# Key blocks taken from the group right ahead, u loaded through another queue, and result banks in pairs: one change to a kernel of gated attention and experts

## The chip, the cores and the metric

The kernel runs on one core of a Trainium2 chip. The metric is the device time of one execution in microseconds (us). The time before is the median of three executions, 911.72 us (906.89 to 917.02). The execution that the profiler recorded is a separate one; its span is 944.3 us.

## The reference

Eight sequences of 2816 tokens go through a gated attention without softmax, and every token then through a dense two-layer net plus one of eight experts, chosen by a gate:

```python
scores = scale * np.matmul(z, z.transpose(0, 2, 1))     # z: 8 x 2816 x 64, scale = 1/2816
attn = np.maximum(scores, 0.0) ** 2
x = u * np.matmul(attn, v)                              # u, v: 8 x 2816 x 256
...
h_dense = np.maximum(x @ w1_dense, 0.0)                 # 256 -> 512
y_dense = h_dense @ w2_dense                            # 512 -> 256
expert_idx = np.argmax(x @ w_gate, axis=1)              # 8 experts
y_moe[mask] = gate_w[mask, None] * (np.maximum(x[mask] @ w1[e], 0.0) @ w2[e])
out = y_dense + y_moe
```

The scores are z times its own transpose. So the score of query i and key j is that of query j and key i, and a block of the attention matrix is the transpose of the block across the diagonal.

## The kernel before, in words

**Attention.** A sequence is 22 tiles of 128 tokens. Its query tiles are worked in six groups of 2, 4, 4, 4, 4 and 4 tiles (`groups`). For a group n the kernel keeps a buffer `A[n]` that holds, for all 22 key tiles, the squared and clipped scores of the group's queries; there are three such buffers, in turn. A buffer is filled in units. A unit is two key tiles (in groups of four query tiles): two score matmuls on TensorE (L353; 64 rows each, in the two halves of the array), a clip and scaling from PSUM into `r` (L370 on ScalarE or L372 on VectorE) and a square from `r` into `A` (L383 on ScalarE or L385 on VectorE). Units are issued in batches of up to three (`fill`, `scores`), as three PSUM pairs `psS` of two banks each are there for them.

Not all key blocks are computed. For group n the keys of group n - 2 of the same sequence (`far`) are the transposes of blocks that stand in `A[n - 2]` already, and are moved from there by DMA transposes on the Sync queue (`far_steps`, L414): one for each query tile of the target, 128 x 512 values at the most. `left[n]` lists the units that remain.

`av` then forms the products of one query tile with v: 22 matmuls of 128 x 256 (L486) into one of two single PSUM banks (`psY`). Between them it issues batches of scores for this group and the two next, and at three places in a tile it may issue one transpose from the list `turning`, if the planner reckons that its source is there. `gate_x` multiplies the result by u (L508, VectorE) into `pays` and starts a DMA transpose of it (L510, Sync queue), which the gate's logits need.

**The order.** TensorE, ScalarE, VectorE and the Sync queue run in the order in which the program issues to them. A small planner in the program picks that order: it keeps a clock `now`, assumed durations for each operation, and gives each clip and square to whichever of ScalarE and VectorE it reckons to be done first. GpSimd's order is left to the framework.

**Queues.** Loads of u (L140, 256 KB for two tiles) are on the Sync queue, as are all transposes. GpSimd issues the loads of v, of z (from the second sequence on) and of the weights, and the scatter of every tile's rows into a table `xs` sorted by expert (L620). A tile's rows in `pays` can be overwritten only once their scatter, 22 tiles earlier, has landed.

**Expert slots.** After attention come up to 92 slots of 256 tokens (`slot`). The first 70 (`NT1`) have one expert for all 256 tokens, the later ones one for each half. The last two are run only if the routing needs them. A slot s does, in this order on TensorE: the dense up-product of its tokens, the down-products of the second half of slot s - 2, its expert's up-product, and the down-products of the first half of slot s - 1 (`up`, L823; `half` and `down`, L831). ScalarE evicts up-products through a relu (L825). A half's two results, dense and expert, share one PSUM bank: the dense one is copied out (L843 on VectorE in the first 70 slots, L845 on ScalarE later), then VectorE adds the scaled expert one (L846), and GpSimd scatters the sum to the output (L848). `expert` copies the weights of the next slot's expert next to each other (L809, VectorE).

In this half all eight PSUM banks are one ring (`bank`): an up-product takes two banks, one for each pair of hidden chunks, each with a relu of its own; a half takes one bank. The attention's PSUM pools are closed before it (`part1`).

Of the kernel before, what the change touches and what calls it, by code (L numbers as in the profile page):

```python
# [15 lines left out]
P = 128  # L16
# [3 lines left out]
def kernel(  # L20
# [58 lines left out]

    part1 = ctx.enter_context(ExitStack())  # L80
    psS = part1.enter_context(tc.tile_pool(name="psS", bufs=NPAIR, space=bass.MemoryType.PSUM))
    psY = part1.enter_context(tc.tile_pool(name="psY", bufs=2, space=bass.MemoryType.PSUM))
    psR = []

    def bank():
        if not psR:
            part1.close()
            psR.append(pool("psR", 8, space=bass.MemoryType.PSUM))
        return psR[0].tile([P, 4 * P], F32, name="bank", tag="b")[:]
# [47 lines left out]
    def load_u(g):  # L137
        ut = aw.tile([P, 2, D], F32, name="ut", bufs=3)
        b, i = divmod(g, nK)
        nc.sync.dma_start(out=ut[:], in_=uf[:, b, i:i + 2, :])  # L140
        ut_of[g], ut_of[g + 1] = ut[:, 0, :], ut[:, 1, :]
# [177 lines left out]
    left, far, key_at = {}, {}, {}  # L319
    for n, (b, i0, w) in enumerate(groups):  # L320
        far[n] = [m for m in (n - 2,) if m >= 0 and groups[m][0] == b]
        turned = {k for m in far[n] for k in range(groups[m][1], groups[m][1] + groups[m][2])}
        ks = [k for k in range(0, nK, 2) if k not in turned]

        left[n] = [tuple(ks[x:x + 4 // w]) for x in range(0, len(ks), 4 // w)]
# [78 lines left out]
    def far_steps(a):  # L404

        n = a + 2
        if n >= len(groups) or far[n] != [a]:
            return []
        (b, i0, w), (_, j0, wj) = groups[n], groups[a]

        def step(i):
            assert n - 1 in A
            open_group(n)
            nc.sync.dma_start_transpose(out=A[n][:, j0:j0 + wj, i * P:(i + 1) * P],  # L414
                                        in_=A[a][:, i0 + i, :wj * P])
            if i == w - 1:
                for j in range(wj):
                    key_at[n, j0 + j] = now[0] + 10.0

        return [(a, lambda i=i: step(i)) for i in range(w)]  # L420
# [50 lines left out]
    def av(n, i):  # L471
# [7 lines left out]
        for x in range(nK):  # L479
            k = rest[0]  # L480
            if i == i0:

                k = min(rest, key=lambda k: (key_at.get((n, k), 9e9), k))
                need(n, k)
            rest.remove(k)
            nc.tensor.matmul(out=o[:], lhsT=A[n][:, k, (i - i0) * P:(i - i0 + 1) * P],  # L486
                             rhs=v_of[b][:, k, :], start=(x == 0), stop=(x == nK - 1))
            pe(0.1092)
            if x % 2 == 1:
                fill(n)  # L490
            if x % 7 == 3 and turning:
                t = can_turn(turning[0][0] + 2, turning[0][0])
                if t is not None and t <= now[0] and turning[0][0] + 1 in A:
                    turning.pop(0)[1]()
            if x == nK // 2 and b * nK + i > Q1 * G:
                one_scatter()
# [21 lines left out]
    def logits(q):  # L518
        n = sizes[q]
        if psR:  # L520
            lg = bank()[:, :G * E].rearrange("p (t e) -> p t e", e=E)
        else:
            lg = psS.tile([P, G, E], F32, name="lg", tag="s")
        lg_of[q] = lg[:, :n, :]
        for j in range(n):
            xT = xT_of.pop(starts[q] + j)
            for c in range(2):
                nc.tensor.matmul(out=lg[:, j, :], lhsT=xT[:, c, :],
                                 rhs=wg[:, c, :], start=(c == 0), stop=(c == 1))
# [24 lines left out]
    def route_pre(q):  # L554
        oh, ex = rs[q]
        if psR:
            pre = bank().rearrange("p (i x) -> p i x", i=2)
        else:
            pre = psS.tile([P, 2, E * G], F32, name="pre", tag="s")
# [253 lines left out]
    def up(xT, ws):  # L813

        n = 2 // len(ws)
        h = take("h")
        for f2 in range(2):
            h_ps = bank().rearrange("p (f h t) -> p f h t", f=2, h=2)
            for i, w1 in enumerate(ws):
                hs = slice(i * n, (i + 1) * n)  # L820
                for f in range(2):
                    for c in range(2):
                        nc.tensor.matmul(out=h_ps[:, f, hs, :], lhsT=w1(c, 2 * f2 + f),  # L823
                                         rhs=xT[:, hs, c, :], start=(c == 0), stop=(c == 1))
            nc.scalar.activation(h[:, 2 * f2:2 * f2 + 2, :],  # L825
                                 h_ps.rearrange("p f h t -> p f (h t)"), AF.Relu)
# [7 lines left out]
    def half(s, j):  # L834
# [4 lines left out]
        y = bank().rearrange("p (k d) -> p k d", d=D)  # L839
        down(y, 0, hd, lambda f: w2d[:, f, :], j)  # L840
        down(y, 1, he, lambda f: we[:, 2 * F + f * D:2 * F + (f + 1) * D], j)
        if s < NT1:
            nc.vector.tensor_copy(yd, y[:, 0, :])  # L843
        else:
            nc.scalar.copy(yd, y[:, 0, :])  # L845
# [21 lines left out]
    def slot(s, end):  # L867
# [12 lines left out]
        if s + 1 < NT and s + 1 not in wes:  # L880
# [129 lines left out]
    for s in range(NT - MAYBE + 2):  # L1010
# [4 lines left out]
        if s % 3 == 1:  # L1015
# [5 lines left out]
    with tc.If(n > NH - 2 * MAYBE):  # L1021
        for s in range(NT - MAYBE, NT + 2):
# [31 lines left out]
```

## Time and profile before

Busy time of the engines over the span of 944.3 us:

| engine | busy us | share | instructions |
|---|---|---|---|
| TensorE, matmuls (PE) | 901.0 | 95% | 8298 |
| TensorE, weight loads (PEld) | 698.5 | 74% | 8298 |
| VectorE (DVE) | 769.7 | 82% | 1563 |
| ScalarE (ACT) | 707.3 | 75% | 950 |
| GpSimd (POOL) | 464.8 | 49% | 434 |

The hardware queue, which Sync's transfers use, moved 67.37 MB in 221664 packets, the software queue of GpSimd 55.44 MB in 27616. The page gives a share for a whole span, though the two halves differ: attention runs from 11.6 to 585.9 us, the slots from 586.7 us on. So shares are best asked for by stretch. A group's line gives the line of the program, the engine, what is written from what, the number of instructions, busy us and the mean of one in ns, and after the bar the idle time just before them with what ended most of it. Matmuls overlap in the array, so the mean of one (274 ns for L486) is its latency; the distance from one to the next, a median of 109 ns, is read from the timeline.

### The profile page before, as it was taken

The numbers are of one execution on the slowest core, as the hardware profiler recorded it, in microseconds if no ns is written. First come the engines' busy times: TensorE is split into PE (matmuls) and PEld (weight loads), VectorE is DVE, ScalarE is ACT, GpSimd is POOL, SyncE is SP. The second block draws the span as 40 slices with busy tenths as digits, with TensorE's granted clock in tenths as the row PEclk, the third lists the DMA queues.
The fourth block names the chain that finished last, engine by engine and source line by source line (L and its number), as shares of the span: only waits on it lengthen the run. The fifth ranks groups of instructions, "written<-read, shape, count | busy, mean of one in ns | idle before, by whom it ended". The sixth has DMA issues, their size and how long they took to land.

```text
span 944.3 us, 23155 instructions
## 1 busy us (share of the span) xinstructions
PE 901.0 (95%) x8298; PEld 698.5 (74%) x8298; DVE 769.7 (82%) x1563; ACT 707.3 (75%) x950; POOL 464.8 (49%) x434
## 2 busy tenths in 40 slices
PE   8999999999999999999999999988998999999996
PEld 5677776767777777777777767877777888888885
DVE  7999998988998998998998985766775776676555
ACT  7998997987987988987988972545554655566764
POOL 2202544445544555554455454556655555556555
PEclk8999999999999999999999999999999999999998
DMA  6687799888797999789798563555543444344332
GB/s 142 127 140 140 138 189 147 145 167 159 144 156 156 148 170 168 141 159 173 133 176 159 125 132 84 106 126 117 114 99 103 111 110 114 101 97 102 90 90 65
DMA packets 249395, 124.28 MB, mean 132 GB/s; under 512 B 217022, under 2 KB 224446, under 8 KB 249280
## 3 DMA queue, kind: packets, MB, share of 16 engines
q1 hardware_dynamic: 221664, 67.37, 37.6%
q0 software_dynamic: 27616, 55.44, 28.6%
q8 instruction: 65, 1.06, 0.5%
q14 instruction: 50, 0.41, 0.2%
HBM read 61.54 MB, written 37.16 MB: 105 GB/s over the span
## 4 chain that ended last, share of the span: by engine, by line
PE 42%; issue 22%; DVE 14%; POOL 13%; DMA 6%; ACT 1%; POOLq 1%; SPq 1%; DVEq 0%; ACTq 0%
PE o L486 21%; PE bank L823 8%; POOL out_dram L848 8%; PE s L353 6%; PE bank L831 5%; DMA xs<-pays,pi 4%; POOL xs L620 4%; DVE r L372 3%; DVE A L385 3%; DVE pays L508 2%; DVE ring L809 1%; DVE ring L843 1%; DMA A<-A 1%; DVE zn L116 1%; DVE ring L846 1%
## 5 line engine op out<-in xcount | busy, mean ns | idle before, releaser
L486 PE MATMUL o<-vb,A 128*128 128x256 bf16 x3872 | 457.2, 274 | 6.8 <-DVE pays L508 3.6
L486 PEld LDWEIGHTS <-A 128*128 128x128 bf16 x3872 | 365.1, 98 | 108.0 <-issue 63.6
L620 POOL DMA_INDIRECT xs<-pays,pi x176 | 230.6, 1310 | 264.6 <-DVE pi L619 145.2
L370 ACT ACTIVATE r<-s 128x1024 f32<-128x1024 f32 x292 | 280.6, 1010 | 48.0 <-PE s L353 33.9
L825 ACT ACTIVATE ring<-bank 128x512 bf16<-128x512 f32 x360 | 193.7, 609 | 141.7 <-PE bank L823 100.5
L383 ACT ACTIVATE A<-r 128x1024 bf16<-128x1024 f32 (+1 forms) x235 | 238.4, 1047 | 12.2 <-DVE r L372 9.3
L385 DVE TENSOR_TENSOR A<-r 128x1024 bf16<-128x1024 f32 x197 | 235.4, 1214 | 0.6 <-ACT r L370 0.6
L848 POOL DMA_INDIRECT out_dram<-ring,me x140 | 146.5, 1046 | 111.6 <-DVE ring L846 72.8
L372 DVE TENSOR_SCALAR r<-s 128x1024 f32<-128x1024 f32 x140 | 170.2, 1218 | 7.8 <-PE s L353 5.2
L831 PEld LDWEIGHTS <-ring 128*128 128x128 bf16 x1440 | 139.7, 98 | 20.0 <-issue 3.9
L353 PE MATMUL s<-zT 64*128 64x512 bf16 (+1 forms) x944 | 122.6, 364 | 4.3 <-ACT zT L183 2.2
L843 DVE COPY ring<-bank 128x256 f32<-128x256 f32 x140 | 58.3, 416 | 70.3 <-PE bank L823 66.2
L823 PE MATMUL bank<-ring 128*128 128x256 bf16 (+1 forms) x880 | 98.5, 255 | 15.6 <-DVE ring L809 6.2
L846 DVE SCALAR_TENSOR_TENSOR ring<-bank,me,ring 128x256 f32<-128x256 f32 x180 | 86.9, 483 | 28.5 <-ACT ring L845 23.1
L831 PE MATMUL bank<-w2d,ring 128*128 128x256 bf16 x720 | 108.3, 273 | 1.9 <-ACT ring L825 1.0
L831 PE MATMUL bank<-ring 128*128 128x256 bf16 x720 | 108.0, 273 | 0.4 <-issue 0.4
L508 DVE TENSOR_TENSOR pays<-o,ut 128x256 bf16<-128x256 f32 x176 | 74.4, 423 | 30.2 <-DMA xs<-pays,pi 15.3
L823 PEld LDWEIGHTS <-ring 128*128 128x128 bf16 x880 | 70.6, 98 | 37.8 <-DVE ring L809 20.5
L823 PE MATMUL bank<-ring,w1d 128*128 128x256 bf16 x720 | 94.5, 274 | 1.8 <-issue 1.2
L809 DVE COPY ring<-wall 128x2048 bf16 x114 | 84.6, 758 | 12.9 <-issue 11.6
L823 PEld LDWEIGHTS <-w1d 128*128 128x128 bf16 x720 | 70.2, 98 | 10.8 <-issue 2.4
L353 PEld LDWEIGHTS <-zT 64*128 64x128 bf16 x944 | 35.8, 94 | 54.9 <-issue 36.9
(121 smaller groups left out, 294.6 us busy)
## 6 DMA issues: line engine op xcount, KB each, us to landing
ut<-in_u_dram SPq DMA_DIRECT2D x88, 256.0 KB
vb<-in_v_dram POOLq DMA_DIRECT2D x16, 384.0 KB
vb<-in_v_dram POOLq DMA_DIRECT2D x16, 320.0 KB
wall<-in_moe_w_dram POOLq DMA_DIRECT2D x16, 256.0 KB
xT<-pays SPq DMA_TRANSPOSE x176
xs<-pays,pi POOLq DMA_INDIRECT x176
zr<-in_z_dram POOLq DMA_DIRECT2D x7, 352.0 KB
out_dram<-ring,me POOLq DMA_INDIRECT x140
```

The lines of the kernel that those rows point to most:

```text
L353: nc.tensor.matmul(out=s[:, h, x * c:(x + 1) * c], lhsT=zT[r, k + h, :], rhs=zT[r, i0:i0 + w, :], start=True, stop=True)
L370: nc.scalar.activation(r[:, :, :c], s[:, :, :c], AF.Relu, scale=1.0 / S)
L372: nc.vector.tensor_scalar(out=r[:, :, :c], in0=s[:, :, :c], scalar1=1.0 / S, scalar2=0.0, op0=ALU.mult, op1=ALU.max)
L383: nc.scalar.activation(a, r, AF.Square)
L385: nc.vector.tensor_mul(a, r, r)
L486: nc.tensor.matmul(out=o[:], lhsT=A[n][:, k, (i - i0) * P:(i - i0 + 1) * P], rhs=v_of[b][:, k, :], start=(x == 0), stop=(x == nK - 1))
L620: ins = nc.gpsimd.indirect_dma_start(out=xs, out_offset=bass.IndirectOffsetOnAxis(ap=pi[:], axis=0), in_=pays[:, g % (2 * G), :].bitcast(F ...
L823: nc.tensor.matmul(out=h_ps[:, f, hs, :], lhsT=w1(c, 2 * f2 + f), rhs=xT[:, hs, c, :], start=(c == 0), stop=(c == 1))
L825: nc.scalar.activation(h[:, 2 * f2:2 * f2 + 2, :], h_ps.rearrange("p f h t -> p f (h t)"), AF.Relu)
L831: nc.tensor.matmul(out=y[:, k, :], lhsT=h[:, f, j * P:(j + 1) * P], rhs=w2(f), start=(f == 0), stop=(f == 3))
L846: nc.vector.scalar_tensor_tensor(out=ys, in0=y[:, 1, :], scalar=me[:, j, 0:1], in1=yd, op0=ALU.mult, op1=ALU.add)
L848: ins = nc.gpsimd.indirect_dma_start(out=out, out_offset=bass.IndirectOffsetOnAxis(ap=ids[j], axis=0), in_=ys, in_offset=None, bounds_chec ...
```

## The change

It has four parts.

- In the last six of the eight sequences, groups 3 and 5 take the keys of the group right ahead (n - 1) from transposes too, beside those of group n - 2. They then compute seven units instead of nine. The group ahead computes the blocks that are wanted first (`ks.sort`).
- In these sequences u is loaded by GpSimd instead of Sync.
- In the expert slots the ring of eight banks goes. Up-products take a PSUM pair from the three of attention and one relu of 128 x 1024; a half takes one of the two single banks. The dense result is always copied out by ScalarE.
- The scatters that are left over after attention are issued in every second slot instead of every third, and the weights of slots that may not run are copied only if they do.

It is meant to spare TensorE, ScalarE and VectorE scores that exist already, to make room for the added transposes on the Sync queue, and to have fewer, larger evictions.

```diff
-    part1 = ctx.enter_context(ExitStack())
-    psS = part1.enter_context(tc.tile_pool(name="psS", bufs=NPAIR, space=bass.MemoryType.PSUM))
-    psY = part1.enter_context(tc.tile_pool(name="psY", bufs=2, space=bass.MemoryType.PSUM))
...
+    psS = pool("psS", NPAIR, space=bass.MemoryType.PSUM)
+    psY = pool("psY", 2, space=bass.MemoryType.PSUM)
...
-        nc.sync.dma_start(out=ut[:], in_=uf[:, b, i:i + 2, :])
+        (nc.gpsimd if b >= 2 else nc.sync).dma_start(out=ut[:], in_=uf[:, b, i:i + 2, :])
...
+    def near(n):
+        b = groups[n][0] if n < len(groups) else -1
+        return groups[n - 1][0] == b and (b >= 2 and n % 6 in (3, 5))
...
-        far[n] = [m for m in (n - 2,) if m >= 0 and groups[m][0] == b]
+        far[n] = [m for m in ((n - 2, n - 1) if near(n) else (n - 2,))
+                  if m >= 0 and groups[m][0] == b]
...
+        if w == 4 and near(n + 1):
+            i1, w1 = groups[n + 1][1:]
+            ks.sort(key=lambda k: (not i1 <= k < i1 + w1, k))
...
     def far_steps(a):
         n = a + 2
-        if n >= len(groups) or far[n] != [a]:
-            return []
...
+        steps = []
+        if n < len(groups):
+            for m in (a, a + 1):
+                if m in far[n]:
+                    steps += [(m, n, lambda m=m, i=i: step(m, n, i)) for i in range(groups[n][2])]
...
     def up(xT, ws):
+        h_ps = psS.tile([P, 4, 2, P], F32, name="h_ps", tag="s")
...
-        for f2 in range(2):
-            h_ps = bank().rearrange("p (f h t) -> p f h t", f=2, h=2)
...
-            nc.scalar.activation(h[:, 2 * f2:2 * f2 + 2, :],
-                                 h_ps.rearrange("p f h t -> p f (h t)"), AF.Relu)
+        nc.scalar.activation(h, h_ps[:].rearrange("p f h t -> p f (h t)"), AF.Relu)
...
-        y = bank().rearrange("p (k d) -> p k d", d=D)
+        y = psY.tile([P, 2, D], F32, name="yy", tag="y")
...
-        if s < NT1:
-            nc.vector.tensor_copy(yd, y[:, 0, :])
-        else:
-            nc.scalar.copy(yd, y[:, 0, :])
+        nc.scalar.copy(yd, y[:, 0, :])
...
-        if s + 1 < NT and s + 1 not in wes:
+        if s + 1 < end:
             wes[s + 1] = expert(s + 1)
...
-        if s % 3 == 1:
+        if s % 2 == 1:
             one_scatter(dve=False)
```

In the changed kernel some lines have other numbers: the products are L491, the key transposes L419, the up-products L822, the dense copy L841, the sum L842 and the weight copy L810.

## The prediction

> **What bounds the kernel now.** I read the busy shares by stretch first, then the groups, then the timeline of one tile in each half, then the waits. The run falls in two halves: attention until 585.8 us, where the first expert matmul follows, and the expert slots after it. Columns of the stretches: length, then busy us (x instructions) of the tensor engine, its weight loads, DVE, ACT and POOL, the clock, the DMA share, GB/s.
> ```profile
> 304.00:374.00 70.00, 70.00 (x655) 51.62 (x653) 65.95 (x127) 62.75 (x69) 35.83 (x30) 1.00 0.95 161
> 374.00:445.00 71.00, 69.95 (x651) 51.26 (x650) 65.51 (x127) 61.98 (x69) 34.96 (x30) 1.00 0.82 155
> 586.00:729.00 143.00, 128.27 (x1129) 107.68 (x1128) 97.12 (x250) 75.17 (x142) 84.47 (x80) 0.99 0.49 110
> 729.00:829.00 100.00, 98.63 (x882) 84.74 (x881) 69.16 (x139) 57.94 (x110) 56.03 (x56) 1.00 0.42 108
> ```
> Two sequences of attention: PE is busy in all of the 70 us, while DVE (94%) and ACT (89%) are nearly full too, and the DMA engines at 82 to 95%. In the expert half DVE and ACT have room, and PE idles only early on. One tile of attention:
> ```profile
> 306.28 0.82 PE L353 MATMUL s<-zT 64*128 64x512 bf16 x6
> 307.03 2.14 PE L486 MATMUL o<-vb,A 128*128 128x256 bf16 x18
> 309.11 0.82 PE L353 MATMUL s<-zT 64*128 64x512 bf16 x6
> ```
> A batch of six score matmuls (three units) pushes the product back from 306.28 to 307.03: 0.75 us a batch, 0.25 us a unit; the product runs on without a gap. So attention is bound by what PE executes, and only matmuls taken off PE shorten it. The groups that I price with:
> ```profile
> L370 ACT ACTIVATE r<-s 128x1024 f32<-128x1024 f32 x292 | 280.6, 1010 | 48.0 <-PE s L353 33.9
> L825 ACT ACTIVATE ring<-bank 128x512 bf16<-128x512 f32 x360 | 193.7, 609 | 141.7 <-PE bank L823 100.5
> L843 DVE COPY ring<-bank 128x256 f32<-128x256 f32 x140 | 58.3, 416 | 70.3 <-PE bank L823 66.2
> L809 DVE COPY ring<-wall 128x2048 bf16 x114 | 84.6, 758 | 12.9 <-issue 11.6
> ```
> In the expert half the first matmuls of slots start at 586.73 and, the last, at 928.72: 342.0 us for 89 slots, 3.84 us each. A slot is 32 matmuls; undisturbed, one follows the other in 3.50 us (800.25 to 803.75). The rest comes from this:
> ```profile
> 802.91 0.42 DVE L843 COPY ring<-bank 128x256 f32<-128x256 f32 x1 [1.81 <-PE bank L823]
> 803.02 3.04 ACT L825 ACTIVATE ring<-bank 128x512 bf16<-128x512 f32 x6 [1.78 <-PE bank L823]
> 804.71 0.92 DVE L809 COPY ring<-wall 128x2048 bf16 x1
> 805.68 0.77 PEld L823 LDWEIGHTS <-ring 128*128 128x128 bf16 x8 [0.31 <-DVE ring L809]
> ```
> DVE and ACT both stand for 1.8 us although the products that they read were issued long before, and are let go together: word of finished matmuls reaches them late. DVE then has two copies and two sums to do before the weight copy (L809), and PE waits 0.31 us for that. Over the run, weight loads waited 20.5 us for L809. Now 89 x 0.34 us = 30 us, and the profiled span, 944.3, is 33 us above the unprofiled median of 911.7. My estimate from these two numbers is that unprofiled slots lie near 3.50 us and that the late releases belong mostly to the profiled run. So I expect little to be won there.
>
> **What the Trainium skill says.** "DMA: Bandwidth & Descriptors", section "DMA Transpose (X-bar)": the plain transpose is issued only from Sync or Scalar; so the new ones lengthen the Sync queue that all transposes here use. The same page, "Issuing engines are not separate DMA queues": issuing from several engines uses the same 16 DMA engines and saves only sequencer time. The trace agrees as far as it goes: both kinds of queue add up to the DMA row (37.6% and 28.6%). "PSUM — Partial Sum Buffer", "Specifications": eight banks of 2 KiB a partition. Three pairs and two singles use all eight, as eight in one ring do, so only the rotation changes.
>
> **The change, part by part.**
> *Scores taken from a transpose.* In six sequences groups 3 and 5 drop two units each: 24 units, 48 matmuls, and each sequence has 18 batches instead of 19. PE: 24 x 0.25 = 6.0 us; with another 0.15 us for each of the 6 batches that vanish (the estimate behind 0.9 us between tiles with and without a batch, 3.3 and 2.4 us), up to 7.2. This is on the path. ACT and DVE lose 24 x (1.01 + 1.05 to 1.22 + 1.21) = 50 to 58 us together, which lies beside PE: nothing on the path, except that the few waits of PE and products for them shrink. I take 1 us.
> *The transposes added.* 48 of 128 KB. The Sync queue took a median 1.264 us for one of this line: 61 us. It loses 66 loads of u at a median 0.524: 35 us. Net +26 us on 425 us, where that queue issues for about 42 of every 50 us. Data: 6.3 of the hardware queues' 67.4 MB at 37.6% of 944 us is 33 us of all 16 engines, 39 us if counted in 256-byte packets; the share rises from 0.87 to about 0.95. Queued behind each transpose are the transposes of x (L510), which the logits need six tiles later, and further key blocks. In tiles 0 to 13 of a sequence Sync has some 14 x 1.2 + 24 x 1.26 + 3 = 50 us to issue in about 43, and tiles 14 to 21 add none of these, so it falls some 7 us behind and recovers. A near block is issued in the group two ahead of its use: four tiles or 12 us, and these keys are taken last in the first tile. 7 + 2 us fits, with 3 us over. Cost 0, at worst 1 us for each of 12 groups.
> *u through GpSimd.* 66 issues; the trace has none of u there. Nearest rows: v loads 586 ns, weight loads 809. So 39 to 53 us on POOL, which is busy for 35 of 70 us: hidden. It also waits for DVE's gating of the tile before (L508), and the scatters stand behind it; who waits for those is the gating 22 tiles later, where DVE now waits 15.3 us in all. At most a tile's delay: 0 to 2 us.
> *Paired banks.* Per slot ACT had four times 0.609 = 2.44 us. Now two evictions at 1.01 (L370's size) and two copies at 0.394 (the late slots' own): 2.81 us of 3.50, no longer than PE. DVE loses 2 x 0.416 us. The result bank: two banks where eight rotated. ACT copy, then DVE sum, are done about 2.1 us after the end of the dense up-product; the bank is wanted 3.5 us after it. So 1.4 us of slack where before it was about 3. Without late releases: 0.
> *The end.* The copies for slots that do not run go: 932.51 and 935.31, 1.45 and 1.48 us on DVE ahead of the last sums, behind which ACT waited 1.87 us. Worth 1.5 us. The closing of the first PSUM pools goes: the first expert matmul waited 0.53 us for the last gating; 0.5 us. Scatters every second slot: POOL has over a us free in a slot; 0.
>
> Sum: -6.0 to -7.2, -1, -1.5, -0.5, +0 to +2: about -9.5, and 911.7 becomes 902.
>
> **The rivals.**
> *Weights come earlier.* If part of the 0.34 us a slot is also lost unprofiled, DVE, relieved by 0.83 us a slot, frees L809 sooner. For it: 20.5 us of waits. Half back is 10 us: 892.
> *The two result banks bind.* If late releases exist unprofiled too: one that ends at 802.9 lets ACT copy until 803.3 and DVE sum until 803.8, while the product for that bank was issued at 802.87: PE loses 0.9 us instead of 0.3. If half of the 45 such events (one in two slots) meet the bank, 22 x 0.6 = 13, and ACT's longer chain to the weight copy adds some 5: slower by 18, less the 9 won: 921. Against it: the 33 us between profiled and unprofiled.
> *The transposes eat it.* Sync at over 90% and DMA at 0.95 make keys or x late: 12 groups x 0.75 = 9: 911, no change. Against it: ACT waited for a key block's transpose only 2.6 us in all.
>
> **How the numbers follow.** Forecast (902) 0.50, earlier weights 0.17, banks 0.16, transposes 0.17. The forecast lies near the 1% line at 902.6; I put 0.32 of its 0.50 beyond it, as the runs before scatter by 10 us. Faster 0.32 + 0.17 = 0.49, same 0.18 + 0.17 = 0.35, slower 0.16. The range runs from the first rival's 892 to 918, short of the second rival's end.
>
> **What would show it.** Right: six batches and 48 score matmuls fewer, sequences 2 to 7 about 1.2 us shorter each, PE still full there, ACT and DVE down to about 85%; slots near 3.5 to 3.8 us as before, few waits of PE for L841 or L842's banks. Wrong: PE waiting before L491 on a transpose, Sync busy without a gap over whole sequences, gatings waiting for u; or slots above 3.9 us with PE waiting for DVE's sum. The step that I trust least is that late releases are the profile's own.

## The result, and the profile after

The changed kernel takes 964.45 us (962.07 to 978.56), the kernel before 910.85 us (906.89 to 917.02) beside it: ratio 1.057, interval 1.050 to 1.065. One of the four executions, the one of 978.56, fell in a slower state and is not in the ratio. The prediction was 902 us, so it is wrong in direction as well as in size. The profiled run of the changed kernel has a span of 962.0 us.

First the stretches, in the columns of the prediction: five sequences of attention (numbers 2 to 6, counted from 0), and the expert slots.
```profile
161.00:242.70 81.70, 70.54 (x642) 52.00 (x640) 63.27 (x126) 56.85 (x62) 37.17 (x41) 0.94 0.90 147
242.70:318.70 76.00, 69.68 (x643) 51.24 (x644) 63.42 (x125) 57.20 (x63) 39.28 (x41) 1.00 0.92 161
318.70:402.80 84.10, 72.19 (x643) 52.53 (x644) 63.52 (x127) 56.93 (x63) 38.98 (x41) 0.92 0.81 146
402.80:482.80 80.00, 72.49 (x644) 52.82 (x644) 64.23 (x127) 56.93 (x63) 39.54 (x41) 0.96 0.85 151
482.80:564.00 81.20, 71.88 (x643) 52.32 (x642) 63.14 (x125) 56.72 (x62) 38.32 (x40) 0.94 0.87 150
630.00:942.00 312.00, 310.00 (x3002) 279.45 (x3000) 174.22 (x379) 228.01 (x354) 207.68 (x188) 1.00 0.49 116
```
The eight score matmuls fewer per sequence are there (642 to 644 where there were 651 to 655), and still PE's busy time has not fallen, while a sequence lasts 76 to 84 us where it lasted 70 to 71. So PE, which had been busy in all of a sequence, now stands in it for 6 to 12 us. The slots are the opposite: PE is busy in 310.0 of 312.0 us, one slot every 3.49 us in the first 70 and 3.51 later (medians). Nearly all that was lost was lost in attention, which ends at 630 us and not at 586.

The rest is at the very end. The program closes with a drain on GpSimd. Here are GpSimd's drains in the kernel before and in the changed one (shortest/median/longest in ns, then first and last start):
```profile
L1049 POOLq DRAIN  x3: 46/115/3733, 939.7 to 944.0; - x3
L1046 POOLq DRAIN  x3: 46/109/8398, 952.8 to 961.7; - x3
```
From the last landing of a transfer to the end of the run, 9.2 us pass where it was 2.2, so this costs about 7 us. In all six profiles of this document in which GpSimd loads u, the longest drain takes 8.4 to 9.6 us; in the fourteen others it takes 2.5 to 4.0. So it comes with the loads of u on GpSimd. Why the drain grows is not shown.

Cut up by tile (counted from 0), most of the loss sits in tile 14, the first of group 4. It takes 16.0, 7.4, 17.0, 5.5 and 14.7 us in these sequences and 3.3 us before: 44 of the 50 us that the five sequences lose. Only the fourth of them loses more elsewhere (2 of its 9 us in tile 14, 5 in tile 7). Here is the first of them, in the timeline (start, duration, queue or engine; in brackets how long the engine had stood, and what let it go):
```profile
203.29 3.21 SPq L110 DMA_TRANSPOSE zT<-zn  x1
206.47 0.82 PE L355 MATMUL s<-zT 64*128 64x256 bf16 x11
210.92 4.46 SPq L419 DMA_TRANSPOSE A<-A  x2
211.75 0.42 DVE L515 TENSOR_TENSOR pays<-o,ut 128x256 bf16<-128x256 f32 x1 [4.77 <-DMA xs<-pays,pi]
217.22 0.39 PE L355 MATMUL s<-zT 64*128 64x256 bf16 x1 [9.93 <-DMA zT<-zn]
217.55 3.81 PE L491 MATMUL o<-vb,A 128*128 128x256 bf16 x18
219.45 2.36 DVE L387 TENSOR_TENSOR A<-r 128x1024 bf16<-128x1024 f32 x2 [6.08 <-DMA A<-A]
```
These score matmuls belong to the next sequence. Eleven of a batch of twelve run at 206.47; the twelfth is the first to read the second half of the next sequence's zT, and stands 9.93 us for the DMA transpose that Sync had issued at 203.29. Products of this sequence, whose data are all there, are queued behind it. VectorE then stands in its turn for the scatter that must free a row of `pays`, and for transposes out of the buffer A that the next sequence will write.

Over the run, the waits (us in total, times, longest):
```profile
DVE pays L515 <- DMA xs<-pays,pi: 40.7, 17, 4.8
PE s L355 <- DMA zT<-zn: 31.2, 6, 9.9
DVE A L387 <- DMA A<-A: 11.6, 2, 6.1
```
The first was 15.3 us before; the other two are not among the thirty largest waits of the kernel before. All three are waits for a landing. Each transfer ends in 16 completion events, so its landing can be read from the trace; from issue to the last of the 16, around that stall:
```
issue   what                        us to landing
194.97  transpose of x                2.4
196.26  zT, first half                4.7
202.03  key transpose                 8.3
203.29  zT, second half              13.9
206.55  key transpose                12.8
208.55  transpose of x               12.7
222.85  transpose of x                2.8
```
GpSimd issues five loads of u, v and weights between 196.1 and 206.7; among them a transpose of x takes 12.7 us to land, five times as long as the one at 194.97.

### The profile page after: what moved, and what is told of

The parts are those of the page before. It is cut to its first block, busy times and chain, and to the rows that moved or that the text cites. A ratio compares the mean times of both kernels' runs of the same rounds, so it can differ in the third digit from the quotient of the medians.

```text
span 962.0 us, 22806 instructions
## 1 busy us (share of the span) xinstructions
PE 890.4 (93%) x8250; PEld 705.4 (73%) x8250; DVE 698.5 (73%) x1411; ACT 703.1 (73%) x870; POOL 494.7 (51%) x500
## 4 chain that ended last, share of the span: by engine, by line
PE 42%; issue 20%; DVE 15%; POOL 12%; DMA 8%; ACT 1%; POOLq 0%; DVEq 0%; SPq 0%; ACTq 0%
PE o L491 18%; PE h_ps L822 9%; PE yy L830 9%; POOL out_dram L844 8%; DVE r L374 6%; PE s L355 5%; DMA xs<-pays,pi 4%; DVE A L387 4%; POOL xs L621 3%; DVE pays L515 2%; DMA out_dram<-ring,ix 1%; DMA vb<-in_v_dram 1%; POOL ut L131 1%; POOL vb L123 1%; DMA ut<-in_u_dram 1%
## 5 line engine op out<-in xcount | busy, mean ns | idle before, releaser
L491 PE MATMUL o<-vb,A 128*128 128x256 bf16 x3872 | 463.9, 276 | 7.7 <-DVE pays L515 2.7
L491 PEld LDWEIGHTS <-A 128*128 128x128 bf16 x3872 | 369.2, 99 | 110.0 <-issue 62.4
L372 ACT ACTIVATE r<-s 128x1024 f32<-128x1024 f32 x265 | 256.7, 1016 | 83.9 <-PE s L355 80.5
L825 ACT ACTIVATE ring<-h_ps 128x1024 bf16<-128x1024 f32 x180 | 184.0, 1023 | 92.2 <-PE h_ps L822 91.2
L385 ACT ACTIVATE A<-r 128x1024 bf16<-128x1024 f32 x222 | 226.1, 1052 | 25.0 <-DVE r L374 20.9
L387 DVE TENSOR_TENSOR A<-r 128x1024 bf16<-128x1024 f32 (+1 forms) x186 | 219.4, 1199 | 19.1 <-DMA A<-A 11.6
L842 DVE SCALAR_TENSOR_TENSOR ring<-yy,me,ring 128x256 f32<-128x256 f32 x180 | 86.9, 483 | 133.8 <-ACT ring L841 130.2
L830 PE MATMUL yy<-w2d,ring 128*128 128x256 bf16 x720 | 108.0, 273 | 0.1
L830 PE MATMUL yy<-ring 128*128 128x256 bf16 x720 | 108.0, 273 | 0.0
L131 POOL DMA_DIRECT2D ut<-in_u_dram x66 | 37.7, 572 | 131.8 <-DVE pi L620 63.8
L822 PE MATMUL h_ps<-ring,w1d 128*128 128x256 bf16 x720 | 93.3, 273 | 2.0 <-DMA ring<-xs 1.9
L822 PE MATMUL h_ps<-ring 128*128 128x256 bf16 (+1 forms) x880 | 93.7, 253 | 0.0
L810 DVE COPY ring<-wall 128x2048 bf16 x110 | 76.9, 714 | 6.0 <-issue 4.6
L822 PEld LDWEIGHTS <-ring 128*128 128x128 bf16 x880 | 74.4, 98 | 6.8
L822 PEld LDWEIGHTS <-w1d 128*128 128x128 bf16 x720 | 70.2, 98 | 10.3 <-DMA ring<-xs 2.1
```

Source lines behind the costliest of these rows:

```text
L372: nc.scalar.activation(r[:, :, :c], s[:, :, :c], AF.Relu, scale=1.0 / S)
L385: nc.scalar.activation(a, r, AF.Square)
L387: nc.vector.tensor_mul(a, r, r)
L822: nc.tensor.matmul(out=h_ps[:, f, hs, :], lhsT=w1(c, f), rhs=xT[:, hs, c, :], start=(c == 0), stop=(c == 1))
L825: nc.scalar.activation(h, h_ps[:].rearrange("p f h t -> p f (h t)"), AF.Relu)
L830: nc.tensor.matmul(out=y[:, k, :], lhsT=h[:, f, j * P:(j + 1) * P], rhs=w2(f), start=(f == 0), stop=(f == 3))
```

## The experiments

Each group of runs has its own measurement of the kernel before, and these lie near 911 us or between 945 and 954 us, depending on the group. The groups ran on different chips (two of them on the same). So all figures below are ratios to the kernel before of the same group. Theory 1 was that the added transposes stand in Sync's queue and in the DMA engines ahead of the next sequence's z. Variant 1a blames Sync's issue rate, 1b the DMA engines' load. Theory 2 blames u on GpSimd's queue, theory 3 the banks.

**One part at a time.** Each is the kernel before with one part of the change. `n_only` has the change's `near`, `far`, `ks.sort` and `far_steps`, with u on Sync and the ring of eight banks. `banks_only` is the changed kernel without these two parts: the paired banks, and with them the copies on ScalarE, the scatters in every second slot and the spared weight copies. `u_only` is one line:
```diff
-        nc.sync.dma_start(out=ut[:], in_=uf[:, b, i:i + 2, :])
+        (nc.gpsimd if b >= 2 else nc.sync).dma_start(out=ut[:], in_=uf[:, b, i:i + 2, :])
```


> The kernel before with one part of the change alone: groups 3 and 5 of the last six sequences take the keys of the group right ahead from transposes; u stays on the Sync queue, the ring of eight banks stays. Theory 1 (the next sequence's transposed z comes too late, because the added transposes stand before it in the Sync queue and in the DMA engines, and the products reach it sooner): this part alone costs most of the 53 us, 940 to 970 us, with TensorE waiting 4 to 10 us for zT in tile 14 of a sequence. Theory 2 (u's loads on GpSimd hold up the scatters and through them VectorE): about 905 us, six us faster than before. Theory 3 (the paired banks): 905 us.

> The kernel before with u loaded by GpSimd in the last six sequences and nothing else. Theory 1: within 5 us of before, 906 to 916 us, since the Sync queue only gets shorter. Theory 2: 940 to 965 us, with VectorE waiting some 30 us for landed scatters, as in the changed kernel (40.7 us against 15.3). Theory 3: 911 us.

> The changed kernel with its first two parts undone: no keys of the group right ahead, u on the Sync queue; paired banks, ScalarE's copies, scatters in every second slot and the spared weight copies stay. Theories 1 and 2: 905 to 911 us; the profile's expert half at 3.5 us a slot as in the changed kernel, where the profile of before had 3.84. Theory 3: 940 us or more.


Near keys alone: 995.42 us, ratio 1.052 (1.047 to 1.058). u alone: 962.37, 1.016 (1.010 to 1.023). Banks alone: 943.05, 0.995 (0.992 to 0.998). So the keys carry the loss, u adds to it, and the banks with the other edits of the slots win a little. Of the near keys alone, and then of u alone, from the waits:
```profile
PE s L364 <- DMA zT<-zn: 48.2, 10, 9.9
DVE A L396 <- DMA A<-A: 32.4, 6, 9.4
```
```profile
POOL ut L140 <- DVE pi L619: 61.5, 36, 4.1
DVE pays L508 <- DMA xs<-pays,pi: 30.1, 20, 3.9
```
With near keys, TensorE's waits for zT are larger than in the whole change, since all loads of u are on Sync too: the second half of zT is issued 9 to 11 us after the first, where it was 5 to 6 before. With u on GpSimd and no near keys there is no wait for zT. GpSimd's load of u stands for VectorE instead (61.5 us), the scatters queue behind it, and VectorE's wait for scatters doubles from 15.3 to 30.1 us. Of the 17 us that u costs alone, some 6 are the longer drain at the end (8.1 us from the last landing to the end, 2.2 before).

The banks were run again, with more rounds, to see whether their gain holds.


> Before with the paired banks, the copies on ScalarE and the other expert edits alone, a second time. It had 0.995 where expert slots of the kernel before lasted 3.83 us. If the gain lies in the expert slots' late releases, it is gone where slots last 3.49: 0.999 to 1.001; if in the attention stage or the end, it stays, 0.993 to 0.997; if TensorE meets the two result banks, 1.002 to 1.01.


942.31 us, 0.997 (0.995 to 0.9995). Where in the run it lies isn't settled: the kernel before was near 947 us in that group too, so the case with slots of 3.49 us wasn't met.

**Issue rate or load.** In the first kernel below four key transposes become one of 512 KB: the same bytes in a quarter of the instructions. `merged_near_banks` is the same with u on Sync, `merged_on_before` merges the 128 key transposes of the kernel before. `no_u` takes the loads of u out of the last six sequences. The edits in part, first for `merged_keys`:
```diff
...
+            if wj == 4:
...
+                nc.sync.dma_start_transpose(
+                    out=A[n][:, j0:j0 + 4, :].rearrange("p j (i q) -> p (j i) q", q=P),
+                    in_=A[m][:, i0:i0 + 4, :].rearrange("p k c -> p (k c)"))
...
```
and for `no_u`, in `load_u`:
```diff
+        b, i = divmod(g, nK)
+        if b >= 2:
+            ut_of[g], ut_of[g + 1] = w2d[:, 0, :], w2d[:, 1, :]
+            return
```


> The changed kernel in full, but the four transposes that bring one group's key blocks to another (four query tiles each) are one instruction of 512 KB: the same blocks and the same bytes, a quarter of the instructions (the products read the blocks in the order in which they then lie). Theory 1a (the Sync queue can't issue so many transposes: about 1.2 us each whatever their size): TensorE's waits for zT go and the time falls by 30 to 60 us, to 0.98 to 1.02 of before. Theory 1b (the DMA engines can't move so many small packets): the bytes are unchanged, so the time stays above 1.04 of before. Theory 2 (u on GpSimd's queue): as 1b.

> Keys of the group right ahead, all key transposes merged four to one, paired banks, but u on the Sync queue. Theory 1a: the six to seven us of scores that are saved come through, without the cost of u on GpSimd: 0.975 to 0.995 of before, the fastest of all. Theory 1b: 1.04 or more. Theory 2: 1.0.

> The kernel before with its own key transposes (those of group n - 2 alone) merged in the same way, four to one, and nothing else. Theory 1a: the Sync queue is relieved by about 12 x 1.2 us a sequence, which was already close to its limit: 0.98 to 1.0 of before. Theory 1b: 1.0, no change.

> The changed kernel without the loads of u in the last six sequences (the gating multiplies by a piece of the dense weights that lies in SBUF, so the output is not the reference's): 16.8 MB less for the DMA engines and 66 issues less for GpSimd, the Sync queue as in the changed kernel. Theory 1a (Sync can't issue so fast): TensorE still waits for zT for 20 us or more, 1.03 to 1.06 of before. Theory 1b (DMA engines full): below 1.01. Theory 2 (u on GpSimd): about 1.04, as only the part that u_only showed goes.


Merged: 1020.82 us, 1.072 (1.067 to 1.077), worse than unmerged. Merged with u on Sync: 994.83, 1.046 (1.041 to 1.052). Merged on the kernel before: 954.31, 1.000 (0.997 to 1.004). Without u: 975.94, 1.026 (1.021 to 1.031). So 1a alone falls. Merging takes Sync's issue time in sequences 2 to 6 from 328.7 to 272.1 us (a merged transpose takes Sync 3.2 us, four single ones 5.0), and nothing is won. 1b alone falls too, as it forecast less than 1.01 without u. The loads of u are worth some three points, twice what `u_only` showed, but `no_u` takes them off GpSimd's queue and off the DMA engines at once and doesn't tell the two apart; TensorE still waits 30.6 us for zT. Nor does zT land sooner by merging: in the merged kernel the second halves of zT are issued in tiles 11 and 12, in time, and land 7.5 to 15.8 us later.

**Sending z earlier.** If zT is late, load and transpose it earlier:
```diff
-            soon(t + 3, lambda b=b: load_z(b + 1))
-            soon(t + 8, lambda b=b: turn_z(b + 1, 0, nK // 2), 0.4)
-            soon(t + 9, lambda b=b: turn_z(b + 1, nK // 2, nK), 0.4)
+            soon(t - 10 if b else 3, lambda b=b: load_z(b + 1))
+            soon(t + 1 if b else 8, lambda b=b: turn_z(b + 1, 0, nK // 2), 0.4)
+            soon(t + 2 if b else 9, lambda b=b: turn_z(b + 1, nK // 2, nK), 0.4)
```


> The changed kernel in full, but the next sequence's z is loaded 13 tiles and turned 7 tiles sooner from the third sequence on, so that its transposes stand ahead of the added ones. Theory 1: TensorE's 31 us of waits for zT go, and 20 to 40 us of the loss with them: 920 to 940 us. Theory 2: within 8 us of the changed kernel, 956 to 970 us.


982.03 us, 1.039 (1.034 to 1.044): of the 5.7 points 1.8 come back, some 17 us, where 20 to 40 were expected. Of its waits:
```profile
DVE A L387 <- DMA A<-A: 44.0, 6, 11.0
ACT A L385 <- DMA A<-A: 39.8, 6, 10.9
```
Nothing waits for zT's transposes now, and the time has gone into the next wait in line: the next sequence's first A buffer is that of group 3, and its last transposes are late as well. Curing one arrival doesn't cure the lateness.

**The two terms of the sum apart.** `drop_only` leaves the 24 units out and adds no transposes. `trans_only` keeps all units and adds transposes only, in four sequences. `near_group3` and `near_group5` split the near keys. In three of these expectations I counted the added transposes wrongly: the traces show 48 for the whole change (176 key transposes where there were 128), 32 in `trans_only`, 24 in each of the two halves.
In turn, against the run with near keys alone:
```diff
-            for m in (a, a + 1):
+            for m in (a,):
...
-            nc.tensor.matmul(out=o[:], lhsT=A[n][:, k, (i - i0) * P:(i - i0 + 1) * P],
+            nc.tensor.matmul(out=o[:], lhsT=A[n][:, k - 4 if near(n) and i0 - 4 <= k < i0 else k, (i - i0) * P:(i - i0 + 1) * P],
```
```diff
-        return groups[n - 1][0] == b and (b >= 2 and n % 6 in (3, 5))
+        return groups[n - 1][0] == b and (2 <= b <= 5 and n % 6 in (3, 5))
...
-        turned = {k for m in far[n] for k in range(groups[m][1], groups[m][1] + groups[m][2])}
+        turned = {k for m in far[n][:1] for k in range(groups[m][1], groups[m][1] + groups[m][2])}
...
+            if m == n - 1:
+                x = spare[0] = (spare[0] + 1) % 4
+                nc.sync.dma_start_transpose(
+                    out=wall[:, 7, x * 4 * P:(x + 1) * 4 * P].rearrange("p (j q) -> p j q", q=P),
+                    in_=A[m][:, i0 + i, :wj * P])
+                return
```
```diff
-        return groups[n - 1][0] == b and (b >= 2 and n % 6 in (3, 5))
+        return groups[n - 1][0] == b and b >= 2 and n % 6 == 3
```
The last is `near_group3`; `near_group5` has `n % 6 == 5`.


> Before, with the 24 score units of the change left out and no transposes in their place: the products of groups 3 and 5 of the last six sequences read the key block four further down instead, so the output isn't the reference's. It measures the gain term alone, and separates two readings of the stall at tile 14. Theory 1 (the next sequence's zT and the A buffers come late because the added transposes stand ahead of them in Sync's queue): nothing is added, so the whole 6 to 7 us are won, ratio 0.992 to 0.995. Rival E (the products come to the next sequence's zT earlier, because 24 units are gone, and stand there whatever Sync does): zT is met one to two tiles early in five sequences, 3 to 5 us each, ratio 1.01 to 1.02.

> Before, all score units kept, with the added transposes as extra work in sequences 3 to 6 (24 of the 36; their destination is a part of the expert weights' tile that is loaded later). It measures the cost term alone. Theory 1: the near-keys run lost 10 to 13 us in each of these sequences against the kernel before, and here at least half of that, 5 to 13 us in each, ratio 1.02 to 1.05, with VectorE, ScalarE or TensorE waiting on transposes of z and of A. Rival E: extra transposes alone find room, ratio 0.998 to 1.004.

> Before with near keys in group 3 alone of the last six sequences (24 of the 36 added transposes, issued in tiles 8 to 13, just ahead of the next sequence's z transposes). Theory 1: these are the ones in the way, so nearly the whole loss of the near-keys run stays, ratio 1.035 to 1.055. If the loss goes by the number of transposes whatever their place: two thirds of 5.2 per cent, 1.035. Rival E: half to two thirds of the units are gone, 1.02 to 1.03.

> Before with near keys in group 5 alone (12 of the 36 added transposes, issued after tile 14, behind the next sequence's z transposes). Theory 1: they are not in z's way, and the loss is gone, ratio 0.993 to 1.003. If the loss goes by the number of transposes: one third, 1.017. Rival E: 1.015 to 1.03, since the products reach the next sequence's z as early as with all units gone.


Units left out and nothing added: 975.38 us, ratio 1.027 (1.022 to 1.033). Transposes alone: 969.51, 1.022 (1.016 to 1.027). Group 3 alone: 995.55, 1.051 (1.045 to 1.058). Group 5 alone: 959.01, 1.011 (1.004 to 1.018). To do less, with nothing in its place, costs 2.7%: that is rival E, and more than it said. But the transposes cost too, as theory 1 has it, and both are needed. `drop_only` has the order of `n_only` on TensorE, matmul for matmul, so the added transposes account for the other 2.5 of the 5.2 points there (the two were measured in different groups). Of the halves, group 3 loses as theory 1 forecast; group 5 lies between theory 1 and rival E, whose branch its interval touches. The loss doesn't go by the number of transposes, as both halves have 24. TensorE in `drop_only`:
```profile
202.86 0.82 PE L364 MATMUL s<-zT 64*128 64x256 bf16 x11
210.96 0.39 PE L364 MATMUL s<-zT 64*128 64x256 bf16 x1 [7.28 <-DMA zT<-zn]
211.29 3.59 PE L502 MATMUL o<-vb,A 128*128 128x256 bf16 x18
```
In TensorE's order the batch that first needs zT's second half comes after two products of tile 14. In the kernel before it comes after 16 products of tile 15 (after 12 in one sequence), over a tile later. The planner lets these scores in as soon as zT's transposes have been issued, once this sequence's own units have run out; with fewer units they run out earlier. The transposes of zT are no earlier; their place follows VectorE's copies, and in this run the second half is even issued 8 us after the first. VectorE waits 22.9 us for A's buffers here too, though no transpose was added.

The kernel before was in time by little: its second halves of zT landed in tile 14 or at the start of 15. And in `trans_only`, where the scores stand exactly as before, the transposes make zT late instead. The stall is then in tile 15:
```profile
283.37 0.39 PE L366 MATMUL s<-zT 64*128 64x256 bf16 x3
289.37 1.24 PE L366 MATMUL s<-zT 64*128 64x256 bf16 x9 [5.61 <-DMA zT<-zn]
290.55 4.54 PE L508 MATMUL o<-vb,A 128*128 128x256 bf16 x26
```
Group 3 has all the loss of the near keys: its transposes stand right ahead of z's, whose second half is issued in tile 14, and the batch comes after four products of that tile. With group 5 it comes after ten, z's second half is issued in tiles 12 and 13, and tile 14 takes 3.4 to 5.5 us; the loss there is mostly one stall, a tile of 15.6 us, for A's buffer.

**Holding the scores back.** If it is the place of the next sequence's scores, moving only these must help. The hold ends at tile 16 in `drop_hold` and `early_hold`, and at tile 17 in the others.
```diff
+    def there(b):
+        return b in z_there and (b < 3 or tile_now[0] >= (b - 1) * nK + 16)
...
-        if groups[m][0] not in z_there:
+        if not there(groups[m][0]):
...
-                if groups[a][0] in z_there and (a == m or m > 0):
+                if there(groups[a][0]) and (a == m or m > 0):
```


> The run without the 24 score units and without added transposes, with one more edit: the scores of the next sequence are held back until tile 16 (in TensorE's order 22 matmuls move from tile 14 to tile 16, all else stays). Groups 3 and 5 read another key block, so the output isn't the reference's. Account A (TensorE stopped because these scores stand ahead of z's landing): the stall of 10 us in each of five sequences goes, less at most 2 us each, ratio to before 0.985 to 1.00. Account B (the order on Sync and VectorE has changed, the wait only shows there): the time comes back in waits on A or on the scatters, ratio 1.015 to 1.03.

> The changed kernel with the scores of the next sequence held back until tile 17. Account A: the stalls at tile 14 (44 us over the five sequences, above the usual 3.3 us) go, and u's 1.6 per cent and some waits of VectorE on scatters stay: ratio 1.005 to 1.03. Account B, or transposes that crowd Sync and the DMA engines wherever the scores stand: 1.04 to 1.06.

> The changed kernel with u back on Sync's queue, and the scores of the next sequence held back until tile 17. Account A: no stall, no cost of u, one unit's gain of 0.5 to 0.7 per cent from the score units and about 0.5 from the paired banks, less small waits: ratio 0.985 to 1.005. Account B, or crowding: Sync's queue is the fullest of all runs here, 1.03 to 1.05.

> The changed kernel with z loaded 13 and turned 7 tiles earlier and the scores of the next sequence held back until tile 16. In the run with early z alone the wait for zT had gone and the wait for A's buffers taken its place (44 us on VectorE, 40 on ScalarE). Account A: two tiles later those buffers are free, ratio 1.005 to 1.025. Crowding: the waits on A stay at 20 us or more, 1.03 to 1.04.


Units left out, scores held: 915.57 us beside 911.45, ratio 1.004 (1.001 to 1.006), from 1.027. The whole change, scores held: 952.34, 1.047 (1.041 to 1.053), from 1.057. With u on Sync: 967.0, 1.059 (1.054 to 1.064). With early z: 945.35, 1.040 (1.033 to 1.046); VectorE and ScalarE still wait 52.6 us for A there. So account A is shown in the main for the units that are left out: 22 matmuls moved by two tiles, with the rest of TensorE's order and all of Sync's unchanged, give back 2.3 of the 2.7 points (the two were measured in different groups). But 1.004 lies just above account A's range, and something of account B is in it: VectorE's waits for scatters rise from 15.0 to 36.8 us. Two sequences of `drop_hold`:
```profile
157.70:230.60 72.90, 69.36 (x644) 51.23 (x645) 62.47 (x125) 57.69 (x63) 31.03 (x30) 1.00 0.88 154
302.30:374.40 72.10, 69.43 (x644) 51.30 (x643) 62.38 (x125) 57.67 (x63) 31.30 (x30) 1.00 0.87 155
```
PE has 69.4 us of work where it had 70.0, and the sequence is still no shorter. In the whole change crowding, the other branch of the expectation, holds. Two sequences of `after_hold`:
```profile
315.20:391.10 75.90, 69.89 (x645) 51.42 (x643) 62.94 (x125) 57.22 (x63) 36.36 (x42) 1.00 0.99 162
466.80:549.90 83.10, 74.38 (x644) 52.79 (x642) 62.58 (x123) 57.63 (x64) 40.86 (x42) 0.94 1.01 148
```
The last column but one is the DMA engines' share: 0.99 and 1.01. It adds up the times of packets from both queues, so 1 is not its limit. Ten microseconds of the kernel before had 1.39, and ten others moved 231 GB/s, the last column:
```profile
145.00:155.00 10.00, 8.14 (x73) 6.03 (x71) 6.06 (x19) 4.22 (x5) 3.31 (x4) 1.00 1.39 168
285.00:295.00 10.00, 9.63 (x105) 7.62 (x103) 7.05 (x17) 5.75 (x8) 4.51 (x5) 1.00 1.26 231
```
So the share says that transfers crowd, not that the engines are full. In `after_hold` the stall at tile 14 is gone (2.4 to 3.0 us), and tiles 15, 17 and 20 take up to 10.7 us instead, with 53.3 us of waits for scatters. (A hold until tile 17 shifts later batches of scores as well: in most sequences six matmuls come in tile 13, where there were none.) With u on Sync that queue has the most to issue of the runs in the last table below (369.8 us), and these are the waits:
```profile
DVE pays L521 <- DMA ut<-in_u_dram: 54.4, 7, 19.7
PE lg L538 <- DMA xT<-pays: 35.2, 7, 15.6
```
u, which that queue carried in time before, now comes up to 19.7 us late, and so do the transposes of x. The last run takes the data of u out of `after_hold`, and leaves Sync's queue and TensorE's order as they are.


> The changed kernel with the scores of the next sequence held back until tile 17 and without the loads of u in the last six sequences (the products are gated by a piece of the dense weights, so the output isn't the reference's). Sync's queue and TensorE's order are those of the run held back until tile 17 with u, which had a ratio of 1.047. If what remained there is the load of the DMA engines (0.97 busy; about 0.78 without u): ratio 0.985 to 1.01. If it is Sync's queue, or the place of the added transposes in it: 1.03 to 1.045.


956.26 us beside 946.62, 1.014 (1.009 to 1.020). Most of what holding back had left goes with the loads of u; the rest is neither nothing nor all, between the two branches. With `no_u` there are now four corners, each from another group and good to 0.5 to 0.8 points:
```
                          u loaded    u not loaded
scores as in the change     1.057        1.026
scores held back            1.047        1.014
```
The place of the scores is worth 1.0 and 1.2 points (the first is hardly clear of the noise), the loads of u 3.1 and 3.3, and 1.4 points remain, which I don't divide further. The points of u hold all that it costs, on GpSimd's queue and in the drain at the end as well as in the DMA engines. `u_only` had 1.6 without near keys, so the two parts of the change make each other dearer. Dropping u isn't a fix, as it has to be loaded.

The two resources in sequences 2 to 6, summed from the traces (issue time on Sync; packet time of the DMA engines over 16), against the 353.4 us that these sequences take in the kernel before (`after` is the changed kernel):
```
                    length   Sync issues   DMA engines
before               353.4      298.0         306.9
n_only               408.0      353.8         336.6
after                403.3      328.7         349.8
after_hold           391.3      330.6         377.6
near_banks_hold      411.6      369.8         365.6
no_u_hold            362.7      323.3         308.0
```
Sync issues one transfer after the other, so with u on Sync its issues alone (353.8 and 369.8 us) fill the 353 us that a run no slower than before would have. That is an estimate, as issues stretch too: zT's second half took Sync 3.21 us above. For the engines the column is no such limit, as the share showed, and it is not a fixed amount of work either: the same transfers took 349.8 us in `after` and 377.6 in `after_hold`. It shows how crowded they are. How much of the loss that crowding makes, apart from the order in which transfers are issued, no run here separates.

## Why the prediction was wrong

*"7 + 2 us fits, with 3 us over. Cost 0, at worst 1 us for each of 12 groups."* Two steps failed, and this is the first: a cost put at nothing. The transposes were held against their own use, four tiles on. What waits for them is queued behind: the transposes of z for the next sequence, and those that still read the A buffer which that sequence writes first. The prediction named the x transposes and "further key blocks" behind each new one, and neither of these two. `trans_only` puts the cost at 20 us for 32 of the 48 transposes (969.51 less 949.83).

*"The share rises from 0.87 to about 0.95."* The direction was right, and 0.95 was then treated as room. The sum left out that u's packets would take longer: the loads of u took 61.7 us of all engines in the last six sequences before, in packets of 2 KB on Sync's queue, and take 75.5 us in packets of 4 KB on GpSimd's. The 256-byte packets went from 130 to 166 us, 36 more, as forecast (33 to 39). In sequences 2 to 6 all packets make 349.8 us, 0.99 of the 353.4 that were to be kept. A share of a whole sequence also doesn't tell when a transfer lands: among five bulk loads, a transpose of x took 12.7 us for 2.4, and zT's second half took 13.9. The trace agrees with what the prediction took from the Trainium skill's "DMA: Bandwidth & Descriptors", section "Issuing engines are not separate DMA queues": with u off Sync the near keys need 240 issues there in five sequences instead of 295, and u's data still meet the transposes.

*"24 x 0.25 = 6.0 us ... This is on the path."* This is the second step that failed: the path. Alone it cost 26 us (`drop_only`, 975.38 less 949.83) where 6 to 7 were to be won. The matmuls did go, and PE's work in an undisturbed sequence fell by 0.6 us (69.4 for 70.0), half of the 1.0 to 1.2 expected. But less work in front only brought TensorE sooner to a batch whose data were not there. The price of a unit was read from a stretch without waits; what it would meet afterwards wasn't followed. With that wait moved away, `drop_hold` still gains nothing (1.004), so the 6 us were never to be had in this order. Whether an order that spreads the held scores better would win them was not tried.

*u through GpSimd, "0 to 2 us".* It measured 1.6%, some 17 us, by the way that the prediction named (scatters queued behind the wait of u's load, VectorE 22 tiles later). VectorE's wait for scatters doubled. But the size was off, and a term was missing: some 6 of the 17 us are GpSimd's longer drain at the end, which the prediction did not have.

*The paired banks, 0; the end and PSUM, -2.* Their sum is about right: together they win 0.3 to 0.5%, 2.5 to 5 us. It was measured only where slots last longer than 3.49 us, and where in the run it lies is not settled. The rival "the two result banks bind" is out for the changed kernel: in slots of 3.49 us PE is busy in 310.0 of 312.0.

*Late releases.* They are not made by profiling as the prediction supposed: `drop_hold`, with the ring of eight banks of the kernel before, has slots of 3.49 us (median) in its profile. The profiles of the groups of runs with 945 us and more show slots of 3.7 to 4.0 us on average, those with 911 us slots of 3.47 to 3.51. The profiled execution of the kernel before has slots of 3.84 us like the former, and its 33 us over the median of 911.7 go with that. So the conclusion that unprofiled slots lie near 3.50 holds for the groups at 911 us, for another reason than the one given.

Of the rivals, "the transposes eat it" had the mechanism (Sync and the DMA engines full, things late), at 9 us. The added transposes cost 20 us for 32 of them, some 24 for all (2.5 points), so it was short by two to three times: it counted one small wait per group, and not that each lateness stops TensorE for 3 to 10 us, with the clock falling on top. It had nothing of TensorE coming to zT sooner. "ACT waited for a key block's transpose only 2.6 us in all" spoke for room that wasn't there: few waits show that all is just in time, not by how much.

## What to carry to other kernels

Before adding work to an in-order queue, list all that stands behind it with its deadline, also of the next outer iteration, and measure from issue to landing when it is busiest: the mean share of 0.87 of the DMA engines hid stretches like the ten microseconds at 1.26, and with 14% more packet time (306.9 us to 349.8) transposes landed late. Taking work away from the engine that sets the pace moves it to its next input sooner; look which input that is and when it lands. And an order that is planned at issue time needs the landing in its plan.

## What I had not expected of the hardware

A stall costs more than its length. After the 9.93 us for zT, 18 products took 3.81 us, 26 took 4.54 after 5.61 us, where 18 take 2.14 and 26 3.01; the granted clock of such sequences is 0.92 to 0.96. The sequence of the changed kernel whose longest wait for zT is 3.15 us keeps 1.00. Around the wait of 9.93 us (TensorE stands from 207.3 us on; the clock is the last column but two):
```profile
207.00:210.00 3.00, 0.29 (x5) 0.01 (x1) 0.00 (x0) 0.98 (x1) 0.26 (x1) 1.00 1.22 132
211.00:221.00 10.00, 3.78 (x18) 2.58 (x19) 3.17 (x5) 2.08 (x2) 1.54 (x2) 0.50 1.15 142
221.00:230.00 9.00, 9.00 (x104) 7.76 (x103) 6.18 (x18) 3.16 (x4) 4.72 (x6) 1.00 1.13 171
```
The Trainium skill's "TensorE: Matmul & The Clock Gate", section "What's actually happening", says that the array falls to half its clock after an idle window of about 3.4 us; the trace agrees: the granted clock is 0.50 from 210.8 to 221.0 us, 3.5 us after TensorE stopped, and the products right after the stall come every 0.21 us instead of every 0.11.

Merging four transposes of 128 KB into one of 512 KB did not make the keys land sooner: in sequences 2 to 6 of the merged kernel the median landing of a merged one is 6.9 us, that of a single one in the changed kernel 4.3, and the small transposes behind took up to 15.9 us.
